# Putting off the first six units' activation, pooling batch 0's keys on TensorE, moving block 1's scaling to GpSimd and batch 1's v pooling among the units

## The chip, the cores and the metric

One core of a Trainium2 chip runs the whole kernel. Its engines are TensorE (PE in the profile, its weight loads PEld), VectorE (DVE), ScalarE (ACT), GpSimd (POOL), and SyncE (SP), whose queue issues nearly all transfers. Each engine works through its own list of instructions in order and waits on semaphores that others raise. The metric is the device time of one execution in microseconds (us).

## What is computed

Three stages in a row, with pooled keys and values in the first:

```
k_p = k.reshape(B, H, Sp, 8, D).mean(axis=3)          # B, H, S, D = 8, 8, 576, 64; Sp = 72
v_p = v.reshape(B, H, Sp, 8, D).mean(axis=3)
attn = softmax(q @ k_p.T / sqrt(D));  x = attn @ v_p  # x: 4608 tokens x 512
h = x @ w_in;  g = h * cos(h);  x = g @ w_out         # w_in 512 x 2048, w_out 2048 x 512
h = x @ w2_in;  s = h * softmax(h);  out = layernorm(s) * g_ln @ w2_out
```

## The kernel before

The tokens are cut into nine blocks of 512 (`NB` = 9, `BLK` = 512; numbered 0 to 8). The program is written out by hand, engine order included: what stands earlier in the code is earlier in each engine's list.

**Beginning.** Before any unit, block 0's attention (`a0`) is run straight through: batch 0's keys are pooled (`add`, L243 to L246: a DVE reduction over eight, and two copies into `kT`), then scores (L426), the exponentials (L441), the scaling by the reciprocal sums (`norm`, L486 and L491), transposes (`e_tr` L522, `e_tr_left` L505) and the products with v (`av`, L549). v of batches 0 and 1 is pooled by matmuls with a 0/1 matrix (`pool_vn`, L287 and L290) and split into parts by `prep_vn`, all before the units.

**Units.** `h = x @ w_in` is made in 72 units, eight to a block. A unit is 24 matmuls (L619) in eight positions of three, into one of three PSUM tiles. Its `chain` has four steps: ACT copies h as a rounded multiple of 2 pi (L630), DVE subtracts that multiple (L633), ACT takes the sine (L636), DVE multiplies by h (L638), which frees the PSUM tile. The steps of a unit run during the next two units; `g_store` then writes the unit to DRAM (`gd`). Among block j-1's units stands block j's attention, at positions that `plan` names, 64 positions to a block: scores and maxima (L391, L399, L400) at 0 to 21, exponentials at 13 and 25, sums and scaling at 16, 19, 28 and 31, the transposes and products from 27 and from 42. The scaling of block 1 (`self.j < 2`) is shared between DVE and POOL, head pair by head pair; later blocks use POOL alone.

**Weights of w_in** arrive as float64 words and are decoded chunk by chunk, 16 chunks, two to a unit of block 0. `pipe.step` does it: ACT prepares (L114, L115), DVE works on the bits (L119, L123, L127), POOL joins them (L139), ACT casts the high part (L1101), POOL subtracts to get the low part (L1102). Through block 0 two steps are run in each unit.

**Last block.** No attention stands among block 8's units. There the weights of the second product are loaded (`w_load`, L856, tiles `ws`) and split by ACT (L163) and POOL (L164); the first two units are read back from `gd` (`g_load`, L653, tiles `gr`), summed (`g_sums`, L664) and split (`g_split`, L675 and L677). The second product (`y_mm`, L702) begins behind the last unit. Its third PSUM bank is the one that the last unit's L638 frees.

Of the kernel before, what the change touches and what calls it, by code (L numbers as in the profile page):

```python
# [19 lines left out]
P = 128  # L20
# [15 lines left out]
def fused_kernel(ctx, tc, qT_d, kT_d, vN_d, vM_d, vL_d, w_in, w_out, w2_in, w2_out, g_ln, out):  # L36
# [183 lines left out]

    def kv_jobs(b, hf):
# [12 lines left out]
        def k_job(i):  # L234
# [45 lines left out]
    def pool_vn(b, hf):  # L280
        if hf == 0:
            pool_vn.ps = ps_y.tile([P, 2, BLK], F32, tag="y", name="vps")
        main, left = pool_vn.ps[:, 0], pool_vn.ps[:, 1]
        t = v_t[b]
        c = slice(4 * D * hf, 4 * D * (hf + 1))
        for i in range(4):
            nc.tensor.matmul(  # L287
                main[:, c], lhsT=pool_w["m"][:, i], rhs=t[i // 2][:, i % 2, c], start=(i == 0),
                stop=(i == 3))
        nc.tensor.matmul(  # L290
            left[:, c], lhsT=pool_w["l"][0:64], rhs=t[2][0:64, 0, c], start=True, stop=True)
        v_t[b, hf] = main, left

    def prep_vn(b, hf):
        main, left = v_t.pop((b, hf))
        vm, vl = vM[b][:, hf], vL[b][:, hf]
        c = slice(4 * D * hf, 4 * D * (hf + 1))
# [3 lines left out]
        nc.vector.tensor_tensor(  # L301
            out=w.rearrange("p (i a d) -> p i a d", i=2, a=2),
            in0=main[:, c].rearrange("p (i a d) -> p i a d", i=2, a=2),
            in1=m_half.rearrange("p (o a u) -> p o a u", o=1, u=1).to_broadcast([P, 2, 2, D]),
            op=ALU.mult,
        )
        for k2, m in enumerate((m_head, m_hlo)):
# [5 lines left out]
        w = w.rearrange("p (i c) -> p i c", i=2)
        nc.scalar.copy(out=vm[:, 0], in_=w)
        nc.scalar.copy(out=hi, in_=u[:, 0])
        nc.gpsimd.tensor_tensor(out=vm[:, 1], in0=w, in1=vm[:, 0].bitcast(F32), op=ALU.subtract)
        nc.vector.scalar_tensor_tensor(
# [1143 lines left out]
```

## Time and profile before

| | |
|---|---|
| device time, median of 3 runs (lowest, highest) | 1356.5 us (1356.32, 1357.1) |
| the profiled execution: device time, span | 1354.56 us, 1352.8 us |
| busy in the span: PE, DVE, ACT, POOL | 1299.7, 1058.2, 697.6, 500.3 us |
| mean granted TensorE clock | 0.988 of full speed |

The span is the time from the first to the last instruction of one execution. Busy times overlap; what counts is where PE has to wait. Units run from 44 us to 563 us of the span, the second product from there to 939 us, the third stage behind it.

### The profile page before, as it was taken

The numbers are of one execution on the slowest core, as the hardware profiler recorded it, in microseconds if no ns is written. First come the engines' busy times: TensorE is split into PE (matmuls) and PEld (weight loads), VectorE is DVE, ScalarE is ACT, GpSimd is POOL, SyncE is SP. The second block draws the span as 40 slices with busy tenths as digits, with TensorE's granted clock in tenths as the row PEclk, the third lists the DMA queues.
The fourth block names the chain that finished last, engine by engine and source line by source line (L and its number), as shares of the span: only waits on it lengthen the run. The fifth ranks groups of instructions, "written<-read, shape, count | busy, mean of one in ns | idle before, by whom it ended". The sixth has DMA issues, their size and how long they took to land. (4 is left out here: it accounts for less than half of the span.)

```text
span 1352.8 us, 20432 instructions
## 1 busy us (share of the span) xinstructions
PE 1299.7 (96%) x7510; PEld 1132.1 (84%) x7510; DVE 1058.2 (78%) x1686; ACT 697.6 (52%) x992; POOL 500.3 (37%) x668
## 2 busy tenths in 40 slices
PE   6879999999999999799999999999999999999998
PEld 4558877887887888699999999999878888888887
DVE  7897887978879684688889999895777767676753
ACT  4576666756557466544444444444444444444432
POOL 3868676665554125230110001001343434343410
PEclk8989999999999999899999999999999999999999
DMA  8425566664665526555455555558501111111101
GB/s 296 155 82 199 192 236 236 236 243 160 236 211 187 185 110 233 183 192 135 148 157 167 164 168 172 160 180 311 191 33 55 39 55 40 55 39 55 40 24 39
DMA packets 81268, 202.93 MB, mean 150 GB/s; under 512 B 7824, under 2 KB 26256, under 8 KB 81168
## 3 DMA queue, kind: packets, MB, share of 16 engines
q1 hardware_dynamic: 81024, 201.62, 44.2%
q8 instruction: 59, 0.97, 0.3%
q14 instruction: 41, 0.34, 0.1%
q10 hardware_dynamic: 144, 0.00, 0.0%
HBM read 124.00 MB, written 77.59 MB: 149 GB/s over the span
## 5 line engine op out<-in xcount | busy, mean ns | idle before, releaser
L619 PE MATMUL h<-x,w 128*128 128x512 f32 x1728 | 435.9, 401 | 1.4 <-DVE t L638 0.8
L702 PE MATMUL y<-g,wy 128*128 128x256 f32 x3024 | 365.8, 284 | 10.9 <-DVE t L638 8.7
L702 PEld LDWEIGHTS y<-g,wy 128*128 128x128 f32 x3024 | 364.8, 193 | 11.9 <-issue 8.8
L619 PEld LDWEIGHTS h<-x,w 128*128 128x128 f32 x1728 | 317.8, 190 | 65.9 <-DVE t L638 1.8
L675 ACT CAST g<-gs 128x1024 fp32r<-128x1024 f32 x72 | 75.7, 1051 | 174.0 <-PE y L702 96.1
L677 DVE TENSOR_TENSOR g<-gs,g 128x1024 fp32r<-128x1024 f32 x72 | 90.2, 1253 | 33.3 <-ACT g L675 33.2
L636 ACT ACTIVATE t<-t,cst 128x1024 f32<-128x1024 f32 x72 | 83.0, 1152 | 63.3 <-DVE t L633 63.2
L139 POOL TENSOR_TENSOR dec<-dec,raw 128x512 int32<-128x512 int32 x24 | 33.9, 1414 | 210.0 <-DVE dec L127 176.4
L638 DVE TENSOR_TENSOR t<-t,h 128x1024 f32<-128x1024 f32 x72 | 87.4, 1214 | 26.1 <-ACT t L636 26.0
L902 POOL TENSOR_TENSOR yl<-yr,yh 128x1024 fp32r<-128x1024 f32 x18 | 43.8, 2433 | 153.5 <-ACT yh L897 153.5
L630 ACT ACTIVATE t<-h 128x1024 int32<-128x1024 f32 x72 | 73.4, 1020 | 49.0 <-PE h L619 48.9
L633 DVE SCALAR_TENSOR_TENSOR t<-t,h 128x1024 f32<-128x1024 int32 x72 | 87.2, 1212 | 5.1 <-ACT t L630 5.1
L231 POOL TENSOR_TENSOR kvraw<-kvraw 128x256 f32<-128x256 f32 (+3 forms) x128 | 82.4, 644 | 9.2 <-DMA kvraw<-in_vM 1.5
L677 DVE TENSOR_TENSOR g<-gr,g 128x768 fp32r<-128x768 f32 x72 | 76.1, 1057 | 0.0
L664 DVE TENSOR_TENSOR gs<-gr,gs 128x256 f32<-128x256 f32 x144 | 71.1, 494 | 5.0
L1033 POOL TENSOR_TENSOR sc<-sc,cst 128x1 f32<-128x1 f32 x36 | 20.3, 564 | 141.5 <-DVE sc L1022 114.1
L1068 ACT COPY o<-o 128x512 f32<-128x512 f32 x36 | 21.1, 587 | 96.4 <-PE o L1086 96.4
L1084 PE MATMUL o<-w,lh 128*128 128x512 f32 x176 | 69.0, 392 | 0.0
L1086 PE MATMUL o<-w,ll 128*128 128x512 f32 x176 | 68.5, 389 | 0.0
L1085 PE MATMUL o<-w,lh 128*128 128x512 f32 x176 | 68.5, 389 | 0.0
L164 POOL TENSOR_TENSOR wy<-ws,wy 128x512 fp32r<-128x512 f32 (+1 forms) x32 | 40.5, 1301 | 61.9 <-ACT wy L163 61.8
L139 POOL TENSOR_TENSOR wf<-dec,raw 128x512 int32<-128x512 int32 x24 | 31.4, 1308 | 83.7 <-DVE dec L127 43.6
(179 smaller groups left out, 2556.7 us busy)
## 6 DMA issues: line engine op xcount, KB each, us to landing
gd<-t SPq DMA_DIRECT2D x72, 512.0 KB, 2.9
gr<-gd SPq DMA_DIRECT2D x72, 512.0 KB, 4.0
raw<-in_w_in SPq DMA_DIRECT2D x24, 512.0 KB, 5.0
raw<-in_w_out SPq DMA_DIRECT2D x24, 512.0 KB, 4.9
kvraw<-in_kT SPq DMA_DIRECT2D x32, 288.0 KB, 4.3
qT<-in_qT SPq DMA_DIRECT2D x36, 256.0 KB, 4.7
yd<-yo SPq DMA_DIRECT2D x36, 256.0 KB, 4.7
yr<-yd SPq DMA_DIRECT2D x18, 512.0 KB, 3.9
```

The costliest lines, as they stand in the source:

```text
L231: nc.gpsimd.tensor_tensor(out=x[:, 0:m], in0=x[:, 0:m], in1=x[:, m:2 * m], op=ALU.add)
L619: nc.tensor.matmul(h_ps[n][:, i], lhsT=w[:, a, kk, :], rhs=x[:, b], start=(kk == 0 and m == 0), stop=(kk == KD - 1 and m == 2),)
L630: nc.scalar.activation(out=t.bitcast(I32), in_=h, func=AF.Copy, scale=1.0 / TWO_PI, bias=0.25)
L633: nc.vector.scalar_tensor_tensor(out=t, in0=t.bitcast(I32), scalar=-TWO_PI, in1=h, op0=ALU.mult, op1=ALU.add)
L636: nc.scalar.activation(out=t, in_=t, func=AF.Sin, bias=halfpi)
L638: nc.vector.tensor_tensor(out=t, in0=t, in1=h, op=ALU.mult)
L664: nc.vector.tensor_tensor(out=o, in0=x, in1=y, op=ALU.subtract)
L675: nc.scalar.copy(out=flat(g[-1])[:, 0:n * NH], in_=flat(f)[:, 0:n * NH])
L677: nc.vector.tensor_tensor(out=flat(g[-1])[:, 0:n * NH], in0=flat(f)[:, 0:n * NH], in1=flat(g[-2])[:, 0:n * NH].bitcast(F32), op=ALU.subtract)
L702: nc.tensor.matmul(y_ps[j][i][:, NH * c:NH * (c + 1)], lhsT=w[:, a, P * c:P * (c + 1)], rhs=g[y][b], start=(q == 0 and c == 0 and k == 0), ...
L1084: nc.tensor.matmul(ps, lhsT=hi, rhs=w[:, 0], start=(c == 0), stop=False)
L1085: nc.tensor.matmul(ps, lhsT=hi, rhs=w[:, 1], start=False, stop=False)
```

## The change

Five edits:

1. Batch 0's keys are pooled by PE: eight matmuls with the identity add up the eight strips of 72 columns in PSUM (a tile of `ps_q`), and DVE copies out of PSUM. The DVE reduction L243 is gone.
2. For units 0 to 5 the four steps of `chain` become one ACT copy from PSUM to a tile, which `g_store` writes to `gd` as plain h. In the last block `put_off` reads each of the six back, does the four steps in SBUF, and writes the result: one load and one store of 512 KB more for each, in two slots of `wo` in turn. Unit n's load stands at position 1 + 8n, its steps 6, 8, 10 and 12 positions behind, its store 14 behind.
3. All of block 1's scaling runs on POOL; in block 0 DVE keeps the odd head pair.
4. `pool_vn` and `prep_vn` of batch 1 leave the beginning. Among block 0's units they stand at positions 1 and 5 (PE), with the DVE, ACT and POOL steps at 3, 4, 6 and 7, 8, 10. Their PSUM tile comes from `ps_a`.
5. In the beginning `e_tr_left(0)` and `e_tr(1)` are written ahead of parts of `norm`.

```diff
             def add():
                 if b == 0:
-                    t = wo.tile([P, SP], F32, "kp")
-                    nc.vector.tensor_reduce(
-                        out=t, in_=raw.rearrange("p (r s) -> p s r", r=POOL), axis=AX.X, op=ALU.add)
+                    if p == 0:
+                        add0.ps = ps_q.tile([P, 2, BLK], F32, tag="q", name="kp")
+                    t = add0.ps[:, 0, SP * p:SP * (p + 1)]
+                    for r in range(POOL):
+                        nc.tensor.matmul(
+                            t, lhsT=ident, rhs=raw[:, SP * r:SP * (r + 1)], start=(r == 0),
+                            stop=(r == POOL - 1))
                     nc.vector.tensor_copy(out=dst[0:D, 0:SP], in_=t[0:D])
...
-                    eng = nc.vector if self.j < 2 and i2 else nc.gpsimd
+                    eng = nc.vector if self.j == 0 and i2 else nc.gpsimd
...
                 for i in range(2):
                     put(i, add, 1, 1, KV[i])
+                    put(1 + 4 * i, pool_vn, 1, i)
+                    staged((3 + 4 * i, 4 + 4 * i, 6 + 4 * i), prep_vn, 1, i)
...
+    NP = 6
+
     def chain(n, step):
+        if n < NP:
+            if step == 0:
+                h_t[n] = gp.tile([P, 2, BLK], F32, tag="t", name="t")
+                nc.scalar.copy(out=flat(h_t[n]), in_=flat(h_ps.pop(n)))
+            return
...
+    def put_off(n, put, o):
+
+        j, q = units[n]
+        t = []
+
+        def load():
+            t.extend(wo.tile([P, 2, BLK], F32, "h", 12 + 2 * (n % 2) + i) for i in range(2))
+            nc.sync.dma_start(out=t[0], in_=gd[j][:, q])
+
+        def step(k):
+            h, g = flat(t[0]), flat(t[1])
+            if k == 0:
+                nc.scalar.activation(
+                    out=g.bitcast(I32), in_=h, func=AF.Copy, scale=1.0 / TWO_PI, bias=0.25)
+            elif k == 1:
+                nc.vector.scalar_tensor_tensor(
+                    out=g, in0=g.bitcast(I32), scalar=-TWO_PI, in1=h, op0=ALU.mult, op1=ALU.add)
+            elif k == 2:
+                nc.scalar.activation(out=g, in_=g, func=AF.Sin, bias=halfpi)
+            else:
+                nc.vector.tensor_tensor(out=g, in0=g, in1=h, op=ALU.mult)
+
+        put(o, load)
+        for k in range(4):
+            put(o + 6 + 2 * k, step, k)
+        put(o + 14, lambda: nc.sync.dma_start(out=gd[j][:, q], in_=t[1]))
...
         pool_vn(0, 0)
         pool_vn(0, 1)
-        prep_vn(0, 0)
+        now(prep_vn(0, 0))
         a0.now("e_tr", 0)
+        a0.now("e_tr_left", 0)
         a0.now("norm", 2)
+        a0.now("e_tr", 1)
+        now(prep_vn(0, 1))
         a0.now("norm", 3)
-        a0.now("e_tr_left", 0)
-        a0.now("e_tr", 1)
-        prep_vn(0, 1)
         a0.now("av", 0)
...
-        pool_vn(1, 0)
         a0.now("e_tr", 3)
         add(1, 0, "k0")
         a0.now("e_tr_left", 1)
-        prep_vn(1, 0)
         a0.now("av", 2)
-        pool_vn(1, 1)
         pipe.step()
-        prep_vn(1, 1)
...
+        for n in range(NP):
+            put_off(n, put_at(NB), 1 + 8 * n)
```

Three places in the engines' lists, in which line numbers shift with the change (L486 and L491, the scaling, become L503 and L508; L1102 becomes L1155; L643, L856 and the chain's L630 and L636 become L669, L909, L656 and L662). First POOL's list at the first scaling in block 0 before the change: joins (`dec`), low parts (`w`), and the even head pair's scaling (`em`, `el`).

```order
L139 TENSOR_TENSOR dec<-dec,raw_163 128x512
L1102 TENSOR_TENSOR w<-dec,w 128x512
L486 TENSOR_TENSOR em<-e,sm 128x4x128
L491 TENSOR_TENSOR el<-e,sm 128x4x32 x2
L139 TENSOR_TENSOR dec<-dec,raw_164 128x512
```

And the same place now:

```order
L139 TENSOR_TENSOR dec<-dec,raw_163 128x512
L1155 TENSOR_TENSOR w<-dec,w 128x512
L503 TENSOR_TENSOR em<-e,sm 128x4x128
L508 TENSOR_TENSOR el<-e,sm 128x4x32 x2
L503 TENSOR_TENSOR em<-e,sm 128x4x128
L508 TENSOR_TENSOR el<-e,sm 128x4x32 x2
L139 TENSOR_TENSOR dec<-dec,raw_164 128x512
```

Both head pairs' scaling now stands in front of the next chunk's join. Next SP's queue in the last block before the change, around the loads of weight pieces 4 and 5 (`ws`) and the stores of units (`gd_119<-t`):

```order
L856 DMA ws<-wf_153 128x1024
L856 DMA ws<-wf_152 128x1024
L643 DMA gd_119<-t 128x1024
L856 DMA ws<-wf_155 128x1024
L856 DMA ws<-wf_154 128x1024
L643 DMA gd_119<-t 128x1024
```

And now, with the put-off loads (`h<-gd_111`) and stores (`gd_111<-h`):

```order
L696 DMA gd_111<-h 128x1024
L909 DMA ws<-wf_153 128x1024
L909 DMA ws<-wf_152 128x1024
L678 DMA h<-gd_111 128x1024
L669 DMA gd_119<-t 128x1024
L696 DMA gd_111<-h 128x1024
L678 DMA h<-gd_111 128x1024
L909 DMA ws<-wf_155 128x1024
L909 DMA ws<-wf_154 128x1024
L669 DMA gd_119<-t 128x1024
L696 DMA gd_111<-h 128x1024
L678 DMA h<-gd_111 128x1024
```

From the first load of weight pieces in the last block to the last row shown there were 18 transfers and are now 28: twelve `ws`, six stores of units, six put-off loads and four put-off stores. Last ACT's list in the last block before the change, one unit and a half of it (`wy` is the weights' split):

```order
L636 ACTIVATE t<-t,cst 128x1024
L630 ACTIVATE t<-h 128x1024
L163 ACTIVATE wy<-ws 128x2x256 x3
L163 ACTIVATE wy<-ws 128x256
L636 ACTIVATE t<-t,cst 128x1024
```

And now, with the put-off first and third steps (L683 and L689) among them:

```order
L662 ACTIVATE t<-t,cst 128x1024
L683 ACTIVATE h<-h 128x1024
L656 ACTIVATE t<-h 128x1024
L163 ACTIVATE wy<-ws 128x2x256 x2
L689 ACTIVATE h<-h,cst 128x1024
L163 ACTIVATE wy<-ws 128x2x256
L163 ACTIVATE wy<-ws 128x256
L662 ACTIVATE t<-t,cst 128x1024
```

The first put-off step, which reads the loaded tile, stands ahead of the next unit's own first step (L656).

## Rows read from the trace of the kernel before

**Rows 1.** Windows: length, busy of PE, PEld, DVE, ACT, POOL; PEclk, DMA share, GB/s

```profile
44.00:121.40 77.40, 62.93 (x288) 49.41 (x289) 67.03 (x94) 48.44 (x70) 58.64 (x66) 0.93 0.40 139
121.40:177.10 55.70, 55.50 (x281) 46.78 (x280) 43.97 (x66) 37.05 (x49) 35.54 (x55) 1.00 0.59 210
519.40:563.20 43.80, 43.80 (x196) 36.28 (x195) 23.12 (x24) 29.28 (x42) 27.04 (x24) 1.00 0.76 260
520.00:550.00 30.00, 30.00 (x134) 24.85 (x133) 14.47 (x12) 22.92 (x36) 23.95 (x22) 1.00 0.98 334
5.40:10.00 4.60, 4.58 (x16) 3.88 (x16) 3.57 (x6) 1.20 (x9) 0.00 (x0) 1.00 1.02 381
```

**Rows 2.** Timeline of PE in block 0: start, length, instructions, [idle before]

```profile
78.24 0.85 PE L522 MATMUL eTp<-ident,em 128*128 128x128 f32 x4 [2.62 <-DVE e L400]
78.74 3.80 PE L619 MATMUL h<-x,w 128*128 128x512 f32 x9
...
87.65 0.66 PE L522 MATMUL eTp<-ident,em 128*128 128x128 f32 x4 [2.60 <-DVE eT L527]
...
93.95 0.52 PE L549 MATMUL xo<-eT,vM 128*128 128x64 f32 x3 [2.27 <-DVE eL L510]
```

**Rows 3.** DVE and POOL groups, 44 to 121.4 us: count | busy us, mean ns

```profile
L633 DVE SCALAR_TENSOR_TENSOR t<-t,h 128x1024 f32<-128x1024 int32 x7 | 8.5, 1211 | 0.0
...
L491 DVE TENSOR_TENSOR el<-e,sm 128x128 f32<-128x128 f32 x4 | 4.0, 1026 | 0.0
...
L486 DVE TENSOR_TENSOR em<-e,sm 128x512 f32<-128x512 f32 x2 | 3.0, 1496 | 0.0
...
L486 POOL TENSOR_TENSOR em<-e,sm 128x512 f32<-128x512 f32 x2 | 2.6, 1289 | 0.0
L491 POOL TENSOR_TENSOR el<-e,sm 128x128 f32<-128x128 f32 x4 | 1.8, 478 | 0.0
```

**Rows 4.** Waits of POOL, 44 to 121.4 us: total us, times, longest

```profile
POOL dec L139 <- DVE dec L127: 14.6, 8, 3.0
```

**Rows 5.** Timeline of ACT in block 0, around the second pair of exponentials

```profile
78.78 0.63 ACT L1101 ACTIVATE w<-dec 128x512 fp32r<-128x512 f32 x1 [0.98 <-POOL dec L139]
80.01 0.70 ACT L114 ACTIVATE dec<-raw 128x512 f32<-128x512 f32 x1 [0.60 <-POOL w L1102]
...
81.32 1.28 ACT L457 ACT_TABLE_LOAD   x1
82.62 1.26 ACT L457 ACTIVATE e<-e 128x576 f32<-128x576 f32 x2
```

**Rows 6.** Timelines of DVE and PE in the beginning

```profile
3.74 1.18 DVE L243 TENSOR_REDUCE kp<-kvraw 128x72 f32<-128x576 f32 x1 [0.16 <-DMA kvraw<-in_kT]
...
5.41 4.58 PE L426 MATMUL sc<-kT,qT 128*128 128x144 f32 x16 [5.41 <-DVE kT L246]
10.62 1.25 PE L426 MATMUL sc<-kT,qT 128*128 128x144 f32 x8 [0.62 <-DVE kT L246]
...
39.62 1.99 PE L287 MATMUL vps<-vn,pool_w 128*128 128x256 f32 x8 [0.50 <-DVE vu L308]
41.54 0.70 PE L290 MATMUL vps<-vn,pool_w 64*128 64x256 f32 x2
...
44.01 0.93 PE L619 MATMUL h<-x,w 128*128 128x512 f32 x3 [0.65 <-DVE vu L308]
```

**Rows 7.** Timeline of ACT in the last block: the first use of a loaded weight piece

```profile
522.01 1.15 ACT L163 ACTIVATE wy<-ws 128x512 fp32r<-128x512 f32 x2 [1.12 <-DMA ws<-wf]
```

**Rows 8.** Timelines of DVE and PE at the end of the last block

```profile
559.89 1.23 DVE L677 TENSOR_TENSOR g<-gs,g 128x1024 fp32r<-128x1024 f32 x1 [2.18 <-ACT g L675]
...
573.33 20.73 PE L702 MATMUL y<-g,wy 128*128 128x256 f32 x158 [8.67 <-DVE t L638]
```

**Rows 9.** Timeline of DVE while POOL splits weights, behind the last block

```profile
591.33 2.32 DVE L677 TENSOR_TENSOR g<-gs,g 128x1024 fp32r<-128x1024 f32 x1
```

**Rows 10.** Groups of DVE instructions, 513 to 565 us

```profile
L638 DVE TENSOR_TENSOR t<-t,h 128x1024 f32<-128x1024 f32 x9 | 11.0, 1218 | 13.8 <-ACT t L636 13.8
```

More of the change, by code (lines that the diff above doesn't have):

```diff
@@ L219, in fused_kernel, with add0 @@
     KV = ("k0", "k1", "v0", "v1", "v2")
+    def add0():
+        pass
     def kv_jobs(b, hf):
@@ L280, in pool_vn @@
     def pool_vn(b, hf):
[L281 to L283 removed]
         t = v_t[b]
         c = slice(4 * D * hf, 4 * D * (hf + 1))
+        if b > 0:
+            ps = ps_a.tile([P, 2, 4 * D], F32, tag="a", name="vps")
+            main, left = ps[:, 0], ps[:, 1]
+        else:
+            if hf == 0:
+                pool_vn.ps = ps_y.tile([P, 2, BLK], F32, tag="y", name="vps")
+            main, left = pool_vn.ps[:, 0, c], pool_vn.ps[:, 1, c]
         for i in range(4):
             nc.tensor.matmul(
[L288 removed]
+                main, lhsT=pool_w["m"][:, i], rhs=t[i // 2][:, i % 2, c], start=(i == 0),
                 stop=(i == 3))
         nc.tensor.matmul(
[L291 removed]
+            left, lhsT=pool_w["l"][0:64], rhs=t[2][0:64, 0, c], start=True, stop=True)
         v_t[b, hf] = main, left
@@ L296, in prep_vn @@
         vm, vl = vM[b][:, hf], vL[b][:, hf]
-        c = slice(4 * D * hf, 4 * D * (hf + 1))
         w = wo.tile([P, 4 * D], F32, "vw")
@@ L300, in prep_vn, with first, second, third @@
         hi = wo.tile([P, 4 * D], F32R, "vh")
[L301 to L307, printed above, removed]
+        w2 = w.rearrange("p (i c) -> p i c", i=2)
+        def first():
             nc.vector.tensor_tensor(
-                out=u[:, k2].rearrange("p (c d) -> p c d", c=4),
-                in0=left[:, c].rearrange("p (c d) -> p c d", c=4),
-                in1=m.rearrange("p (c o) -> p c o", o=1).to_broadcast([P, 4, D]), op=ALU.mult,
-            )
[L313 to L317, printed above, removed]
-            out=vl.rearrange("p i c -> p (i c)"), in0=hi.bitcast(F32), scalar=m_sh, in1=u[:, 1],
-            op0=ALU.mult, op1=ALU.add)
+                out=w.rearrange("p (i a d) -> p i a d", i=2, a=2),
+                in0=main.rearrange("p (i a d) -> p i a d", i=2, a=2),
+                in1=m_half.rearrange("p (o a u) -> p o a u", o=1, u=1).to_broadcast([P, 2, 2, D]),
+                op=ALU.mult,
+            )
+            for k2, m in enumerate((m_head, m_hlo)):
+                nc.vector.tensor_tensor(
+                    out=u[:, k2].rearrange("p (c d) -> p c d", c=4),
+                    in0=left.rearrange("p (c d) -> p c d", c=4),
+                    in1=m.rearrange("p (c o) -> p c o", o=1).to_broadcast([P, 4, D]), op=ALU.mult,
+                )
+        def second():
+            nc.scalar.copy(out=vm[:, 0], in_=w2)
+            nc.scalar.copy(out=hi, in_=u[:, 0])
+        def third():
+            nc.gpsimd.tensor_tensor(out=vm[:, 1], in0=w2, in1=vm[:, 0].bitcast(F32), op=ALU.subtract)
+            nc.vector.scalar_tensor_tensor(
+                out=vl.rearrange("p i c -> p (i c)"), in0=hi.bitcast(F32), scalar=m_sh, in1=u[:, 1],
+                op0=ALU.mult, op1=ALU.add)
+        return first, second, third
     def prep_v(b):
@@ L1104, in c_in, with now @@
         return Chunk(w_in_w[f], done, home)
+    def now(fns):
+        for fn in fns:
+            fn()
     def kv_load(b, hf, *names):
```

2 lines of the change are left out of this document (added).

## Prediction

> **What bounds the kernel now.** I read the stages by windows first, to see where PE is not fed. Units take 55.7 us a block where all goes well: block 1's window is filled by PE to 55.5 us. Block 0 takes 77.4 us for the same 192 matmuls, so 21.7 us are lost there [rows 1]. The last block has no attention and takes 43.8 us with PE busy throughout [rows 1]; behind it PE waits 8.67 us for DVE's last L638 [rows 8]. So the places that the change touches are the first 44 us, block 0's 21.7 us, the last block, which is full, and the wait behind it.
>
> Next the timeline of PE in block 0. The reader is to see waits of 2.3 to 2.6 us, all for DVE [rows 2]: for a score tile that DVE has not read, for a transposed tile (`eT`), for the left part (`eL`). After a wait nine matmuls take 3.80 us where 9 x 43.8 / 192 = 2.05 is the pace; the window's mean granted clock is 0.93, so there are stretches at the lower level of 1.2 GHz, and they follow idle PE. DVE is busy 67.0 of the 77.4 us, POOL 58.6, ACT 48.4 [rows 1]. POOL in turn waits 14.6 us for DVE's bit work before its joins [rows 4]. DVE is the busiest engine of block 0, POOL the next.
>
> In the last block the transfers are the full resource: from 520 to 550 us their share is 0.98 at 334 GB/s [rows 1]. ACT has 29.3 of 43.8 us, DVE 23.1, POOL 27.0.
>
> **The beginning.** Keys: the four DVE reductions of 1.18 us (one is shown) go [rows 6]. In their place PE makes 32 matmuls of 72 columns, which count twice, since the trace records two passes for each fp32 matmul (x16 for eight score instructions). A pass of 144 columns takes 4.58 / 16 = 0.29 us at first and 1.25 / 8 = 0.16 us later [rows 6]; 72 columns lie between half of that and all of it. Sixteen passes for one head pair are thus 2.3 to 4.6 us slow, 1.2 to 2.5 us fast, against 1.18 us on DVE, and the second pair's matmuls, the first copies and the first scores stand in one line on PE. I expect the first scores about 3 us later than at 5.41, and the later ones to catch up, as PE runs on and DVE has 4.7 us less to do. Block 0's v and softmax then run 1 us later or as now. Against that, batch 1's v pooling leaves this stretch: 2 x (1.99 + 0.70) = 5.4 us of PE, and the wait of the first unit for the last read of its PSUM tile, 0.65 us [rows 6]. PE is not full there (5.9 of 8 us just before), so not all of it comes back: I take the first unit 2.4 us earlier. Bounds: 2 us later (pooling slow, nothing regained) and 6 us earlier (all of 5.4 + 0.65).
>
> **Block 0.** Removed from DVE: two operations of 1.21 us in each of six units, 14.5 us, and the odd head pairs' scaling, 3.0 + 4.0 us [rows 3]. So DVE's 67.0 us become about 47. PE gains 5.4 us of v pooling. POOL gains two head pairs' scaling, each 1.29 + 2 x 0.48 = 2.25 us, 4.5 us in all: 63.1 us. That is more than PE's own 55.7 + 5.4 = 61.1 us, so POOL becomes the fullest engine, and block 0 can shrink by at most 77.4 - 61.1 = 16.3 us.
>
> It will shrink by much less, because of where the scaling stands: both pairs are scaled ahead of the next chunk's join, 4.5 us in which no chunk is joined. ACT's cast (L1101) waits for that join, and behind it in ACT's list come the next chunk's preparation, the second pair of exponentials and the transposed tile's cast [rows 5]. So PE's second set of transposes, which now waits until 87.65 [rows 2], still hangs on this chain. Now the join waits for DVE's decode, which stands behind DVE's own scaling (7.0 / 2 = 3.5 us) and a 1.21 us operation of the chain; afterwards it waits for 4.5 us on POOL instead. What is gained there: the table load of 1.28 us [rows 5], since no sine stands between the exponentials, and the chain's operations ahead of the reads of `eT` and `eL`, 1.21 us each; from the waits of 2.60 and 2.27 us [rows 2] I count 2.8 us. Sum 4.1 us: block 0 takes 73.3 us. Bounds: nothing, if POOL's 4.5 us are paid in full twice, and 16.3 us.
>
> **The last block.** Twelve transfers of 512 KB are added to a stage whose transfers are full. In SP's queue 28 instead of 18 stand up to the sixth put-off load (12 weight halves, 6 unit stores, 6 loads, 4 stores). One is 0.524 MB, at 334 GB/s 1.57 us, at the best pace of the beginning, 381 GB/s, 1.38 us [rows 1]. The first landed at 522.0 [rows 7], so the 28th lands 27 x 1.57 = 42.4 us later, at 564.4, or 37.2 us later, at 559.2. The step that reads it stands at position 47 of 64: 519.4 + 47 x 43.8 / 64 = 551.6. It is 7.6 to 12.8 us late; I take 10.5, nearer to the pace of this stage itself. ACT waits at that step with everything behind it: unit 69's first step, and through it the PSUM tile that a later unit needs, the sums and splits of the first units, the last L638. The earlier put-off loads stall PE on the way for the same reason, but that delay is part of this one, not added. At the end DVE had 2.18 us of waiting to spare ahead of the first split [rows 8], and gets one more L638-like operation there, 1.2 us. So the second product begins 10.5 - 2.2 + 1.2 = 9.5 us later, be it as stalls within the block or as a longer wait than 8.67 us behind it. Bounds: 1.2 us if every load is in time, 11.8 us by the slow pace, and 2.2 more if the next paragraph is right.
>
> The operations have another price than in the beginning. With h in PSUM an L638 takes 1.22 us throughout this block, though POOL splits weights beside it for 27 us [rows 1, 10]. A DVE operation of the same size with both inputs in SBUF took 2.32 us beside POOL's splits [rows 9]. The put-off ones have both inputs in SBUF, twelve of them, so up to 12 x 1.1 = 13 us more of DVE, which has 20 us free. Only two stand in the late chain at the end: 2.2 us. The Trainium skill's page SBUF — State Buffer (section Who interferes with whom) says that a DVE instruction with two SBUF inputs and a GpSimd instruction that reads SBUF exclude each other for the whole instruction. By that rule each of the twelve could wait for a whole split; the row just cited agrees in kind. Since the late chain's last operations come when POOL's splits are mostly over, the sum leaves it out.
>
> **The sum.** -2.4 - 4.1 + 9.5 = +3.0 us. Made against the profiled execution's own 1354.56 us it is 1357.6; the median of the runs stands 1.9 us above that execution, so 1356.5 + 3.0 = 1359.5 us. A change of 0.2%, 2.7 us, is about the least that a measurement of this kernel can tell from none.
>
> **Rivals.** (a) *DVE's relief is worth most of block 0's loss.* Every PE wait named in [rows 2] ends on DVE, and DVE loses 20 of 67 us; POOL's waits of 14.6 us for DVE [rows 4] shrink too. If the second exponentials do not hang on the scaling, block 0 falls to 65 us: -2.4 - 12.4 + 9.5 = -5.3, 1351.2 us. It decides at 77.4 - (9.5 - 2.4) = 70.3 us for block 0: below that the kernel is faster. Against it speaks POOL's sum of 63.1 us with its list in order. Chance 0.31.
> (b) *The transfers run at 381 GB/s* [rows 1] *and less is late*: 7.6 - 1.0 = 6.6 us given back, which is 1356.6 us, no change. The best stretch of the beginning is loads alone, the last block mixes stores in. Chance 0.15.
> (c) *The port in the last block*: 2.2 us more, 1361.7 us. Chance 0.10.
> (d) *The beginning gets longer*, since 64 slow passes hold up the first exponentials, and the first unit starts 2 us later instead of 2.4 earlier: 1363.9 us. PE's later passes are at 0.16 us [rows 6], which speaks against it. Chance 0.07.
> The forecast as summed has 0.37.
>
> **Numbers.** Faster comes from (a), 0.29 of its 0.31, and 0.04 of (b) with a somewhat better block 0: 0.33. Slower is 0.27 of the forecast, (c), and 0.05 of (d): 0.42. The rest, 0.25, is within 0.2%. The likeliest case alone spans 1355 to 1364 us. The range must reach through most of (a) and to (d): 1347 to 1367 us.
>
> **What would show it.** Right: block 0 at 72 to 75 us with the first unit near 41.6 us; POOL its fullest engine; PE's longest wait before the transposes in position 33. In the last block ACT waiting for the loads of `h`, in total over 5 us, the block at 46 to 52 us, and L702 resuming some 3 us later than at 573.33. Wrong: block 0 under 70 us; or no ACT wait for `h` loads; or the first scores before 6 us, or the first unit behind 44 us.

## The result and the profile after

| | before | changed |
|---|---|---|
| device time, median of 4 runs each (lowest, highest) | 1356.41 us (1356.2, 1357.1) | 1369.26 us (1368.83, 1373.13) |
| ratio to before, 95% interval | | 1.0104 (1.0091 to 1.0116) |
| profiled execution: device time, span | 1354.56, 1352.8 us | 1373.13, 1371.3 us |

The change makes the kernel 12.9 us slower; 1359.5 was forecast, with 1347 to 1367 as range. The profiled execution of the changed kernel is the longest of its four. A second profile of the same kernel was therefore taken with the experiments (*changed_again*, ratio 1.0113, 1.0098 to 1.0129), and both are read here. The kernel before's profiled execution is 1.9 us below its median, so the spans differ by more than the medians: by 18.5 us in the first profile and 15.4 in the second.

The span falls into five stretches at marks in PE's timeline. Block 0 goes from the first unit's first matmul to the first score matmul that stands among block 1's units (of block 2's attention), blocks 1 to 7 from there to the last product with v, the last block from there until the second product resumes behind its wait for DVE.

| us | before | changed | changed_again |
|---|---|---|---|
| first unit starts | 44.01 | 47.93 | 45.02 |
| block 0 | 78.1 | 78.1 | 78.4 |
| blocks 1 to 7 | 391.5 | 393.3 | 392.4 |
| last block and handover | 59.7 | 73.1 | 73.4 |
| the rest | 779.5 | 778.9 | 778.9 |

So the loss is 1 to 4 us of the beginning and 13.3 to 13.7 us of the last block; block 0, where the change was to pay, is as long as before.

**The beginning.** PE's timeline of the changed kernel: start, length, instructions, [idle before]. The L249 rows are the keys' passes.

```profile
3.88 3.66 PE L249 MATMUL kp<-kvraw,ident 128*128 128x72 f32 x16 [3.88 <-DMA kvraw<-in_kT]
8.11 3.69 PE L249 MATMUL kp<-kvraw,ident 128*128 128x72 f32 x16 [0.57 <-DVE kT L253]
11.59 2.22 PE L443 MATMUL sc<-kT,qT 128*128 128x144 f32 x8
13.60 3.53 PE L249 MATMUL kp<-kvraw,ident 128*128 128x72 f32 x16
...
18.94 2.33 PE L249 MATMUL kp<-kvraw,ident 128*128 128x72 f32 x16
...
28.11 0.66 PE L539 MATMUL eTp<-ident,em 128*128 128x128 f32 x4
...
47.93 1.48 PE L638 MATMUL h<-x,w 128*128 128x512 f32 x3
```

A pass takes 0.22 to 0.23 us in the first three groups. The first scores start at 11.59 us instead of 5.41 [rows 6], and what was meant to catch up does not: PE is busy without a gap from the second group of passes up to the first transposes. In the second profile the third group of passes is faster:

```profile
13.55 2.17 PE L249 MATMUL kp<-kvraw,ident 128*128 128x72 f32 x16
...
25.33 0.66 PE L539 MATMUL eTp<-ident,em 128*128 128x128 f32 x4
```

The transposes then come 2.8 us earlier, and so does the first unit (45.02). The windows show a granted clock of 1.00 over the passes in both profiles, so they do not say why the same passes take 0.22 us (3.53 / 16) in one profile and 0.14 us (2.17 / 16) in the other.

**Block 0.** Windows of the changed kernel over block 0, and over three stretches of the last block (columns as in [rows 1]):

```profile
47.93:126.03 78.10, 68.27 (x313) 53.50 (x311) 59.37 (x85) 42.00 (x67) 66.06 (x73) 0.94 0.44 154
...
525.00:549.00 24.00, 22.69 (x99) 17.89 (x97) 13.16 (x10) 16.72 (x23) 17.21 (x12) 1.00 0.95 329
549.00:555.00 6.00, 0.23 (x1) 0.26 (x2) 2.73 (x3) 3.82 (x5) 1.25 (x2) 0.77 0.97 396
554.70:559.00 4.30, 4.23 (x10) 3.38 (x11) 3.02 (x3) 3.85 (x6) 4.30 (x4) 0.50 0.59 237
```

PE's waits in block 0, which answer to [rows 2]:

```profile
70.36 1.02 PE L408 MATMUL sc<-kT,qT 128*64 128x144 f32 x6 [2.60 <-DVE e L417]
...
93.25 0.66 PE L539 MATMUL eTp<-ident,em 128*128 128x128 f32 x4 [3.23 <-DVE eT L544]
...
98.02 0.59 PE L566 MATMUL xo<-eT,vM 128*128 128x64 f32 x3 [2.02 <-DVE eL L527]
```

The waits at the transposes (2.60 us before) and for `eL` (2.27) still stand. DVE has 59.4 us of work instead of 67.0, not 47. The DVE groups show why, first two of the bit operations on the weights before the change (count | busy us, mean ns | idle before):

```profile
L127 DVE SCALAR_TENSOR_TENSOR dec<-raw,dec 128x512 int32<-128x512 int32 x13 | 10.0, 772 | 0.4
L123 DVE TENSOR_SCALAR dec<-dec 128x512 int32<-128x512 int32 x13 | 9.3, 719 | 0.4
```

and now, with one of the groups that came in with batch 1's v (L333; L321 and L314 took 1.5 and 0.8 us):

```profile
L127 DVE SCALAR_TENSOR_TENSOR dec<-raw,dec 128x512 int32<-128x512 int32 x14 | 15.1, 1075 | 0.5
L123 DVE TENSOR_SCALAR dec<-dec 128x512 int32<-128x512 int32 x13 | 13.0, 998 | 0.4
...
L333 DVE SCALAR_TENSOR_TENSOR vL<-vh,cst,vu 128x256 fp32r<-128x256 f32 x2 | 1.7, 872 | 0.0
```

For thirteen of each that is 13 x (0.303 + 0.279) = 7.6 us more for the same work. With only the scaling moved to POOL (*scaling_alone* below) the means are 833 (L127) and 942 ns (L123), so a part of it comes with POOL's scaling alone. DVE's timeline, one chunk while POOL is idle (it waits from 75.2 to 77.19 us) and the next while POOL works:

```profile
75.81 0.43 DVE L123 TENSOR_SCALAR dec<-dec 128x512 int32<-128x512 int32 x1
76.27 0.69 DVE L127 SCALAR_TENSOR_TENSOR dec<-raw,dec 128x512 int32<-128x512 int32 x1
...
78.81 1.41 DVE L123 TENSOR_SCALAR dec<-dec 128x512 int32<-128x512 int32 x1
80.25 1.42 DVE L127 SCALAR_TENSOR_TENSOR dec<-raw,dec 128x512 int32<-128x512 int32 x1
```

POOL and ACT over the second stretch, which is the chain that the prediction drew:

```profile
79.89 1.22 POOL L503 TENSOR_TENSOR em<-e,sm 128x512 f32<-128x512 f32 x1
...
83.25 0.94 POOL L508 TENSOR_TENSOR el<-e,sm 128x128 f32<-128x128 f32 x2
84.15 1.48 POOL L139 TENSOR_TENSOR dec<-dec,raw 128x512 int32<-128x512 int32 x1
```

```profile
85.66 0.64 ACT L1154 ACTIVATE w<-dec 128x512 fp32r<-128x512 f32 x1 [2.35 <-POOL dec L139]
...
88.52 1.24 ACT L474 ACTIVATE e<-e 128x576 f32<-128x576 f32 x2
89.67 0.56 ACT L543 CAST eT<-eTp 128x512 fp32r<-128x512 f32 x1
```

POOL scales for 4.26 us ahead of the join; ACT's cast, the second exponentials and the cast of the transposed tile follow it, then DVE's part of `eT`, and PE at 93.25.

The slow bit operations are what the Trainium skill's page SBUF — State Buffer (section Who interferes with whom) describes: a DVE instruction with two SBUF inputs, or a `tensor_scalar` in a mode with two ports, and GpSimd shut each other out for the whole instruction. The 0.43 against 1.41 us of L123 agree in kind.

**The last block.** PE's timeline, which answers to [rows 8]:

```profile
542.70 5.72 PE L638 MATMUL h<-x,w 128*128 128x512 f32 x24 [0.73 <-DVE t L664]
554.77 18.64 PE L638 MATMUL h<-x,w 128*128 128x512 f32 x72 [6.35 <-DVE t L664]
573.72 5.72 PE L638 MATMUL h<-x,w 128*128 128x512 f32 x24 [0.30 <-DVE t L664]
...
581.09 1.46 PE L755 MATMUL y<-g,wy 128*128 128x256 f32 x10 [1.42 <-DVE g L730]
592.39 3.97 PE L755 MATMUL y<-g,wy 128*128 128x256 f32 x17 [9.84 <-DVE t L664]
```

SP's queue ahead of the 6.35 us, and ACT with its waits for the first weight piece, the third put-off load and the sixth:

```profile
539.17 0.32 SPq L696 DMA_DIRECT2D gd<-h  x1
540.33 3.29 SPq L909 DMA_DIRECT2D ws<-wf  x2
543.67 0.42 SPq L678 DMA_DIRECT2D h<-gd  x1
```

```profile
527.71 1.16 ACT L163 ACTIVATE wy<-ws 128x512 fp32r<-128x512 f32 x2 [1.08 <-DMA ws<-wf]
...
551.18 1.06 ACT L683 ACTIVATE h<-h 128x1024 int32<-128x1024 f32 x1 [6.18 <-DMA h<-gd]
552.14 1.00 ACT L656 ACTIVATE t<-h 128x1024 int32<-128x1024 f32 x1
...
570.04 1.06 ACT L683 ACTIVATE h<-h 128x1024 int32<-128x1024 f32 x1 [0.46 <-DMA h<-gd]
```

The third put-off load needs the tile that the first put-off unit frees with its L691, which ended at 539.15. Its store leaves at 539.17. The row of 3.29 us behind it is two weight loads, each issued in 0.32 us, and a wait between them: SP waits for POOL's splits of earlier weight pieces (L164) to free the tiles. SP's waits from 539.3 to 544 us (us in total, times, longest):

```profile
SPq L909 <- POOL wy L164: 3.3, 2, 2.6
```

So of the 4.5 us between the store and the put-off load, 3.3 are waits for POOL. The load leaves at 543.67 and lands 7.4 us later. ACT waits 6.18 us with the next unit's L656 behind it, and PE waits for the PSUM tile that this unit's chain frees.

### The profile page after: what moved, and what is told of

Same layout as the page of the kernel before. It is cut to its first block, busy times and chain, and to the rows that moved or that the text cites. A ratio compares the mean times of both kernels' runs of the same rounds, so it can differ in the third digit from the quotient of the medians.

```text
span 1371.3 us, 20603 instructions
## 1 busy us (share of the span) xinstructions
PE 1314.8 (96%) x7574; PEld 1146.8 (84%) x7574; DVE 1058.1 (77%) x1676; ACT 700.7 (51%) x996; POOL 512.1 (37%) x674
## 5 line engine op out<-in xcount | busy, mean ns | idle before, releaser
L638 PEld LDWEIGHTS h<-x,w 128*128 128x128 f32 x1728 | 319.5, 191 | 75.2 <-issue 9.3
L662 ACT ACTIVATE t<-t,cst 128x1024 f32<-128x1024 f32 x66 | 76.0, 1152 | 60.1 <-DVE t L659 59.9
L664 DVE TENSOR_TENSOR t<-t,h 128x1024 f32<-128x1024 f32 x66 | 80.1, 1214 | 13.8 <-ACT t L662 13.8
L656 ACT ACTIVATE t<-h 128x1024 int32<-128x1024 f32 x66 | 67.2, 1018 | 42.8 <-PE h L638 42.8
L659 DVE SCALAR_TENSOR_TENSOR t<-t,h 128x1024 f32<-128x1024 int32 x66 | 80.0, 1212 | 0.0
L717 DVE TENSOR_TENSOR gs<-gr,gs 128x256 f32<-128x256 f32 x144 | 72.1, 501 | 5.0
L730 DVE TENSOR_TENSOR g<-gr,g 128x768 fp32r<-128x768 f32 x72 | 74.5, 1035 | 0.1
L164 POOL TENSOR_TENSOR wy<-ws,wy 128x512 fp32r<-128x512 f32 (+1 forms) x32 | 46.8, 1493 | 68.5 <-ACT wy L163 37.7
```

Of the source, the lines that this page charges most:

```text
L638: nc.tensor.matmul(h_ps[n][:, i], lhsT=w[:, a, kk, :], rhs=x[:, b], start=(kk == 0 and m == 0), stop=(kk == KD - 1 and m == 2),)
L659: nc.vector.scalar_tensor_tensor(out=t, in0=t.bitcast(I32), scalar=-TWO_PI, in1=h, op0=ALU.mult, op1=ALU.add)
L662: nc.scalar.activation(out=t, in_=t, func=AF.Sin, bias=halfpi)
L664: nc.vector.tensor_tensor(out=t, in0=t, in1=h, op=ALU.mult)
L717: nc.vector.tensor_tensor(out=o, in0=x, in1=y, op=ALU.subtract)
L730: nc.vector.tensor_tensor(out=flat(g[-1])[:, 0:n * NH], in0=flat(f)[:, 0:n * NH], in1=flat(g[-2])[:, 0:n * NH].bitcast(F32), op=ALU.subtract)
```

## The experiments

Each kernel's median stands against the kernel before on the same chip. Lengths are those of the table above, from one profile each. Line numbers differ by a few between versions.

| label | median, before, us | ratio (95%) | first unit | block 0 | last block |
|---|---|---|---|---|---|
| keys_dve | 1367.86, 1354.74 | 1.0097 (1.008 to 1.0114) | 42.67 | 78.1 | 74.5 |
| scale_shared | 1369.80, 1354.74 | 1.0116 (1.0101 to 1.0131) | 45.80 | 80.1 | 71.9 |
| no_put_off | 1358.53, 1354.74 | 1.0035 (1.002 to 1.0049) | 47.86 | 80.5 | 59.7 |
| put_off_block7 | 1364.60, 1354.74 | 1.0075 (1.006 to 1.009) | 47.83 | 77.5 | 59.9 |
| changed_again | 1371.05, 1355.68 | 1.0113 (1.0098 to 1.0129) | 45.02 | 78.4 | 73.4 |
| keys_alone | 1359.18, 1355.68 | 1.0029 (1.0018 to 1.004) | 49.11 | 78.8 | 59.7 |
| v_late_alone | 1357.63, 1355.68 | 1.0016 (1.0007 to 1.0026) | 41.23 | 81.5 | 59.8 |
| raw_fix | 1370.77, 1355.68 | 1.011 (1.0095 to 1.0125) | 48.17 | 77.8 | 72.1 |
| two_put_off | 1358.86, 1356.14 | 1.0017 (1.0005 to 1.003) | 45.00 | 79.8 | 61.0 |
| three_put_off | 1363.5 (one run), 1356.14 | | 44.92 | 79.7 | 67.7 |
| spread_alone | 1354.19, 1356.14 | 0.9989 (0.9978 to 1.0) | 44.67 | 75.1 | 59.8 |
| scaling_alone | 1355.64, 1356.14 | 0.9993 (0.9982 to 1.0004) | 45.72 | 76.7 | 59.7 |
| v_late_fix | 1357.91, 1355.90 | 1.0016 (1.0007 to 1.0026) | 41.61 | 81.6 | 59.8 |
| scaling_and_spread | 1353.60, 1355.90 | 0.999 (0.998 to 1.0001) | 44.30 | 74.9 | 59.8 |
| spread_no_keys | 1355.16, 1355.90 | 0.9998 (0.9989 to 1.0007) | 42.16 | 77.8 | 59.8 |

**keys_dve**: from the changed kernel, edit 1 undone.

```diff
-                    if p == 0:
-                        add0.ps = ps_q.tile([P, 2, BLK], F32, tag="q", name="kp")
-                    t = add0.ps[:, 0, SP * p:SP * (p + 1)]
-                    for r in range(POOL):
-                        nc.tensor.matmul(
-                            t, lhsT=ident, rhs=raw[:, SP * r:SP * (r + 1)], start=(r == 0),
-                            stop=(r == POOL - 1))
+                    t = wo.tile([P, SP], F32, "kp")
+                    nc.vector.tensor_reduce(
+                        out=t, in_=raw.rearrange("p (r s) -> p s r", r=POOL), axis=AX.X, op=ALU.add)
```

> The changed kernel with batch 0's keys pooled on DVE again, everything else kept. Theory (the matmul passes of the keys are what delays the beginning): in the changed kernel the key passes took 0.23 us each and the transposes began 6.5 us later than before; without them the first unit starts at 41 to 42 us instead of 47.9, and the kernel takes about 6 us less than the changed one (1363). Rival (the beginning is late because of the waits that follow, the 4.39 us for DVE's x and what was reordered there): the first unit still starts at 45 us or later, and the time falls by less than 3 us.

The first unit starts at 42.67 us, near what the theory has. The time is 13.1 us above before, against 12.9 and 15.4 in the two measurements of the changed kernel, so the 6 us were not there: the rival's size of the gain holds, not its cause. Beside the second profile of the changed kernel (span 1368.2, here 1366.7) 2.3 us come from the first unit and 1.3 from blocks 0 to 7; 1.0 is given back in the last block and 1.1 in the rest. keys_alone shows the edit's price without the others.

**scale_shared**: edit 3 undone.

```diff
-                    eng = nc.vector if self.j == 0 and i2 else nc.gpsimd
+                    eng = nc.vector if self.j < 2 and i2 else nc.gpsimd
```

> The changed kernel with block 1's scaling shared between DVE and POOL again. Theory (the scaling on POOL eats the relief of block 0): in the changed kernel POOL scaled from 79.9 to 84.15 us, the join behind it came late, so did ACT's second exponentials and the transposes, PE waited 3.23 and 2.02 us; with it shared block 0 falls from 77.4 to 72 to 74 us and the kernel takes about 4 us less than the changed one (1365). Rival 1 (DVE's relief is worth nothing, whoever scales): block 0 stays within 1 us of 77.4. Rival 2 (DVE needs the relief of the scaling as well): block 0 gets longer, 79 to 81 us.

The theory falls and rival 2 holds: block 0 is 80.1 us, 1.7 to 2.0 longer. POOL's chain above is real, but sharing the scaling puts as much or more into DVE's list.

**no_put_off**: edit 2 undone.

```diff
-    NP = 6
+    NP = 0
```

> The changed kernel with no unit put off (all six chains where they stood before). Theory: the last block and its handover return to 59.9 us (13.3 us back), and block 0 pays with the chain's twelve DVE operations, 4 to 9 us more than 77.4; together 4 to 9 us faster than the changed kernel (1360 to 1365). Rival (the chain's operations in block 0 were hidden, its length is POOL's): block 0 stays at 77 to 78.5 us and the kernel is 12 to 13 us faster than the changed one, about 1357.

The last block returns to 59.7 us. Block 0 pays 2.1 to 2.4 us, between theory and rival. So the put-off relieves block 0 by some 2.2 us for 14.5 us of DVE work.

**put_off_block7**: the six put-off units' work stands among block 7's units.

```diff
-            put_off(n, put_at(NB), 1 + 8 * n)
+            put_off(n, put_at(NB - 1), 1 + 10 * n)
-            t.extend(wo.tile([P, 2, BLK], F32, "h", 12 + 2 * (n % 2) + i) for i in range(2))
+            t.extend(wo.tile([P, 2, BLK], F32, "h") for i in range(2))
```

> The changed kernel with the six put-off units worked on among block 7's units instead of block 8's, ten positions apart, in the ring of tiles. Theory (the last block's loss is its full transfer queue: the third put-off load is issued late, behind a store and weight loads, and ACT waits 6.18 us for it): in block 7, where the transfers ran at 134 GB/s, no load is late, the last block returns to about 60 us with its handover, block 7 pays at most 2 us, and the kernel takes 11 to 13 us less than the changed one (1356 to 1358). Rival (it is the work itself, 12 ACT and 12 DVE operations in an order that PE waits for): block 7 gets 5 us longer or more, and at most 7 us come back.

The last block returns, but the seven blocks take 400.3 us, 7 to 8 us more than in the changed kernel. The rival holds. Windows of this kernel in block 7:

```profile
490.00:500.00 10.00, 8.16 (x40) 6.15 (x39) 9.83 (x16) 8.15 (x9) 2.85 (x3) 1.00 0.46 171
500.00:510.00 10.00, 7.04 (x27) 5.53 (x26) 9.93 (x13) 6.21 (x9) 5.23 (x6) 0.83 0.73 265
```

DVE is at 9.8 and 9.9 of 10 us, and PE loses 4.8 of 20 us there. With a unit's work every ten positions DVE is the fullest engine; that it sets the length is read from these windows, no run tests it.

**changed_again**: the changed kernel, unaltered.

> The changed kernel once more, unaltered, so that the others of this group stand beside it on one chip: a second profile of it. Theory (TensorE's rise to 2.4 GHz in the beginning comes at different times in different executions): the first unit starts anywhere from 45.5 to 48 us, as it did in the variants so far that share its beginning (45.80, 47.83, 47.86), with block 0 and the last block within 1.5 us of what the first profile showed (78.1 us; 73.1 us from the last product with v to the resumed second product). Rival: it repeats the first profile, 47.9 us.

The first unit starts at 45.02 us, a little ahead of the theory's range and far from the rival's 47.9. The beginnings of the same code stand in two groups, 44.9 to 45.8 and 47.8 to 48.2 us, four profiles in each, by when the passes become faster (13.5 or 18.9 us). The expectation put this down to the level of TensorE's clock; the granted clock is 1.00 there in both profiles, so that is not shown.

**keys_alone**: the kernel before with edit 1 only (its lines as in the diff of the change).

> The kernel before with only the keys of batch 0 pooled on PE. Theory (the passes are slow, 0.23 us each, and delay everything behind the first scores): the first unit starts 3 to 6 us later than 44.0 us and the kernel takes 3 to 6 us more than before, 1358 to 1361 on the clock of the last group's chip. Rival (what is lost in the beginning is caught up in block 0, since undoing this edit in the changed kernel started the first unit 5.3 us earlier, but the kernel got only about 1 us faster): the first unit 3 to 6 us later, block 0 shorter by as much, the time within 1.5 us of before.

The theory holds: first unit at 49.11, 5.1 us late, block 0 not shorter (78.8), the kernel 3.5 us slower. (Single profiles: the beginning of the kernel before stands unaltered in *spread_alone*, *scaling_alone* and *scaling_and_spread* too, and starts the first unit there at 44.67, 45.72 and 44.30 us, so that 3.4 to 5.1 us are late.) So nothing is caught up in block 0.

**v_late_alone**: the kernel before with edits 4 and 5 only.

> The kernel before with only batch 1's v pooled among the units and the order of the beginning that goes with it. Theory (a weight chunk's load on SP waits for the tile that batch 1's v holds until PE has pooled it; q of block 1 is queued behind it): the first unit starts about 1.5 us earlier, at 42 to 43 us, SP waits some 15 us for the pooling, PE waits 3 to 4.5 us for q at the score matmuls of the third head pair, block 0 is 3 to 5 us longer than 78.1, and the kernel is 1 to 4 us slower than before. Rival (SP's queue has time, only 5.4 us of PE move from one place to the other): block 0 at most 2 us longer, the kernel within 1 us of before or faster.

First unit 2.8 us earlier, block 0 3.4 us longer, the kernel 2.0 us slower. The wait of PE for q and SP's wait for the pooling are both there:

```profile
63.65 0.91 PE L401 MATMUL sc<-kT,qT 128*64 128x144 f32 x6 [2.89 <-DMA qT<-in_qT]
```

SP's waits (us in total, times, longest):

```profile
SPq L109 <- PE vps L291: 15.8, 1, 15.8
```

Whether they are the cause is what the next two test.

**raw_fix** (on the changed kernel) and **v_late_fix** (on v_late_alone): the same line.

```diff
-        early = {7: raws[1], 9: raws[2], 11: raws[3]}
+        early = {7: raws[1], 8: raws[2], 9: raws[3]}
```

> The changed kernel with three of the early weight chunks loaded to other tiles (chunks 7, 8 and 9 to the raw tiles that the first chunks leave, 11 to its own), so that none of them waits for the tiles that hold batch 1's v. Theory (SP's queue is held up by that wait of 15.6 us): the two loads of q (L396) are issued before 58 us instead of 63.2 and 64.3, the wait of PE at 70.4 us shrinks by at least 2 us, block 0 falls by 2 to 4 us, and the kernel is 2 to 4 us faster than the changed one. Rival (the chunks behind them, which must be decoded in turn, are late anyway, and POOL's list sets the length): block 0 stays within 1 us and so does the kernel.

The theory falls. The line does not take all of SP's wait away: 6.1 us of waiting for batch 1's pooling are left of 15.6, beside 8.3 us for POOL's joins. SP still issued the loads of q only at 61.66 and 62.61 us, but that was soon enough: PE's wait at the third pair's scores shrinks to 0.80 us. Block 0 stays at 77.8 us, for the wait goes elsewhere:

```profile
68.53 0.91 PE L408 MATMUL sc<-kT,qT 128*64 128x144 f32 x6 [0.80 <-PE h L638]
...
93.22 1.12 PE L539 MATMUL eTp<-ident,em 128*128 128x128 f32 x4 [4.63 <-DVE eT L544]
```

> The kernel before with batch 1's v pooled among the units and with the weight chunks' loads turned so that none waits for the tiles of that v. Theory 1 (the 3.4 us of block 0 are the work that came in: 5.4 us of PE, and on DVE 4 us and slower bit operations): PE's wait for q is gone, but block 0 still is 80 to 82 us, with another wait that has grown; the kernel within 1 us of v_late_alone, 1 to 3 us slower than before. Theory 2 (SP's queue): block 0 falls to 78 to 79 us and the kernel is as fast as before or 1 us faster.

Theory 1 holds. Block 0 is 81.6 us without the wait for q. In its place the wait before the first transposes has grown from 0.59 to 2.60 us; before the second it is 2.84 us (3.36 in v_late_alone). So the late loads of q are not what makes block 0 longer. What is left is the work that came in, 5.4 us of PE and some 4 us of DVE; which of it costs the 3.4 us no run separates.

**two_put_off**, **three_put_off**: `NP = 2` and `NP = 3` in the changed kernel.

> The changed kernel with two units put off instead of six. Theory (the third load is the first that needs a tile which an earlier put-off unit gives back, so it stands in SP's queue behind that unit's store and behind weight loads that go out slowly; with two units there is no such load): PE waits under 1 us within the last block, from the last product with v to the resumed second product 60 to 62 us (73.1 in the changed kernel); block 0 79 to 81 us. The kernel takes 9 to 11 us less than the changed one. Rival (the lateness grows with the amount of transfers, a third of it is a third of the loss): 64 us, and 8 us less.

> The changed kernel with three units put off. Theory (queue order): the whole wait for the third load is there, ACT waits 5 to 7 us for it, PE 4 to 7 us for DVE's last step in the middle of the block, and the stretch from the last product with v to the resumed second product is 66 to 70 us. Rival (the amount of transfers and of work): half of the loss, with no single wait of PE over 3 us, 66 us or less.

With two units PE waits 0.69 us within the block and the last block takes 61.0 us; with three it is 67.7 us. The theory holds in both. PE's timelines, of two, then of three, and ACT's of three:

```profile
538.77 27.48 PE L638 MATMUL h<-x,w 128*128 128x512 f32 x120 [0.69 <-DVE t L664]
```

```profile
549.71 23.56 PE L638 MATMUL h<-x,w 128*128 128x512 f32 x96 [4.78 <-DVE t L664]
```

```profile
546.12 1.06 ACT L683 ACTIVATE h<-h 128x1024 int32<-128x1024 f32 x1 [4.60 <-DMA h<-gd]
```

One more load costs 6.7 us, and ACT waits 4.60 us for it, a little less than expected. The loss does not grow in step with the amount of transfers, it begins with the third load, which stands in the queue behind a store and two weight loads; here too SP waits 3.3 us for POOL between the store and the load. How much of the lateness is that place, and how much the 7 us from issue to landing, no run separates. The other three units cost 5.4 us more between them.

**spread_alone**, **scaling_alone**, **scaling_and_spread**: the kernel before with edit 2, edit 3, and both, the six units placed one in each of blocks 2 to 7.

```diff
+        for n in range(NP):
+            put_off(n, put_at(3 + n), 44)
```

> The kernel before with only the put-off edit, and the six units worked on one in each of blocks 2 to 7, at position 44, instead of all in the last block; their tiles come from the ring. Theory (the relief of block 0 is real, 2.2 us in the changed kernel, and only the place of the work costs): block 0 is 75 to 77 us instead of 78.1, the seven blocks behind it at most 1 us longer, the last block as before; 1 to 3 us faster than before. Rival 1 (DVE's order in the blocks is tight): each of the six blocks is 1 to 1.5 us longer, as block 7 paid 9 us for six units, and the kernel is 4 to 7 us slower. Rival 2: no change, since block 0's length hangs on the decoding of the weights and not on the units' steps.

> The kernel before with only block 1's scaling moved to POOL. Theory (the changed kernel got 1.7 to 2 us longer in block 0 when the scaling was shared again): block 0 is 76 to 77 us instead of 78.1 and the kernel 1 to 2 us faster than before. Rival (POOL's 4.4 us ahead of the next join cost as much as DVE gains as long as the units' steps are still in DVE's list): block 0 within 1 us of 78.1, no change. Rival 2: block 0 is 2 us or more longer, since the second exponentials hang on that join.

> The kernel before with the scaling of block 1 on POOL and the six units put off and spread over blocks 2 to 7. Theory 1 (both take work from DVE and the gains add): block 0 is 73 to 74 us (75.06 and 76.73 alone, 78.1 before), the kernel 2.5 to 4 us faster than before. Theory 2 (POOL's 4.4 us ahead of the next join cost what DVE gains once the units' steps are gone): block 0 75 us or more, the kernel no faster than with the spread alone, 2 us faster than before.

The spread holds block 0 at 75.1 us with the last block as before. The kernel is 2.0 us faster than before by the medians, with an interval that just reaches no change. The seven blocks take 1.2 us more, but so they do in scaling_alone, whose edit does not touch them; this is not shown to be the spread's price. Scaling alone gives 76.7 us in block 0 and no change that can be measured in the time. Together they give 74.9 us: theory 2, the two do not add. POOL is then the fullest engine, and the wait before the second set of transposes has grown:

```profile
44.30:119.15 74.85, 61.11 (x291) 47.77 (x292) 52.46 (x77) 40.17 (x63) 63.77 (x71) 0.98 0.46 156
```

```profile
86.40 1.12 PE L522 MATMUL eTp<-ident,em 128*128 128x128 f32 x4 [4.65 <-DVE eT L527]
```

At 0.999 (0.998 to 1.0001), 2.3 us below before, scaling_and_spread is no faster than spread_alone, and its interval reaches no change as well. None of the kernels here is shown to be faster than before.

**spread_no_keys**: the changed kernel without edit 1, with the spread and with the line of raw_fix.

> The changed kernel without the keys on PE, with the six units spread over blocks 2 to 7 and with the weight chunks' loads turned. Theory (the beginning gains 1.3 to 2.8 us from the late v, block 0 loses what it gains by the rest, the last block is as before): first unit 41 to 42.5 us, block 0 77.5 to 78.5 us, the kernel 1 to 3 us faster than before. Rival (the late v costs as much as it gains): within 1 us of before.

The rival holds: first unit 42.16 us, block 0 77.8 us, the time as before. Beside scaling_and_spread, which lacks edits 4 and 5, the first unit is 2.1 us earlier and block 0 2.9 us longer: what the late v gains ahead of the first unit, it gives back behind it.

## Why the prediction was wrong, by its steps

**The beginning, -2.4 us forecast, +1.0 and +3.9 measured.** The part on batch 1's v was right in size: with edit 5, but without the others, it starts the first unit 2.4 to 2.8 us earlier (v_late_fix, v_late_alone; what edit 5 does by itself no run shows). The step that failed is "the first scores about 3 us later" and "the later ones to catch up, as PE runs on". The passes for two head pairs stand ahead of the first scores, which start 6.2 us later. The keys' 64 passes take 13.2 us of PE in the first profile and 11.4 in the second, all ahead of the first transposes, against four DVE reductions of 1.18 us of which PE waited out only a part. Alone the edit costs 5.1 us at the first unit. This was rival (d), with chance 0.07, on whose account "PE's later passes are at 0.16 us" was held against it; in one of two profiles 48 of the 64 passes were at 0.22 us or more. The first unit behind 44 us, which the prediction named as a sign of being wrong, stands in both.

**Block 0, -4.1 us forecast, 0.0 and +0.3 measured.** The two edits that relieve DVE are worth about what was summed: taking them out of the changed kernel one at a time lengthens block 0 by 2.1 to 2.4 and 1.7 to 2.0 us, and together on the kernel before they give 3.2. What failed is that edit 4's arrival in block 0 had no price. Its 5.4 us of PE stood only in a floor of 61.1 us, and its instructions on DVE, ACT and POOL nowhere. With edit 5 alone beside it, it makes block 0 3.4 us longer, and -3.2 + 3.4 = +0.2 is what was measured. The step "DVE's 67.0 us become about 47" failed too (its own terms, 14.5 + 7.0 off 67.0, make 45.5): it is 59.4 us, 7.6 of the difference because L123 and L127 are slower beside a busier POOL, and 3.5 from v's steps (1.7 + 1.5 + 0.8, less 0.5 that stood there before). Rival (a), with block 0 at 65 us, rested on that figure; no run has block 0 under 74.9 us. The chain from the scaling over the join to the transposes in position 33 was right, and 3.23 us stand there; POOL is the fullest engine of the block behind PE, with 66.1 us.

**The last block, +9.5 us forecast, +13.3 and +13.7 measured.** That loads of `h` come late and ACT holds the next units up behind them was right. The step that failed is which load and why: the sixth of 28 transfers at a given rate was counted, and it is the third, by its place in SP's queue behind a store that waits for the same DVE step as its tile, and behind two weight loads for which SP waits 3.3 us for POOL. The sixth load does land as counted at 334 GB/s, 42.3 us after the first weight half (ACT at 527.71 and 570.04), but that is luck: waits of SP and stretches of 329 and 396 GB/s make it up, and ACT waits only 0.46 us for it. Rival (b), a faster rate, is not tested by any run; its "6.6 us given back" is what would remain of the loss, by which its 1356.6 us is right. PE's waits in the block are 0.73 + 6.35 + 0.30 = 7.4 us. The handover, from the second product's first matmul to its resumption, is 13.1 instead of 10.3 us, 2.8 more, where the forecast had -2.2 + 1.2 = -1.0: DVE has no waiting to spare ahead of its first split any more, and the chain of the last units ends later behind the sums and the put-off steps. Most of the remaining 3 us is PE's pace: after the wait 72 matmuls took 18.64 us where 72 x 0.228 = 16.4 is the pace. The first ten of them, until 559 us, ran at a granted clock of 0.50, which is the lower level of 1.2 GHz, behind the 6.35 us in which PE was idle. The price of a wait in the clock was not in the sum. The units of the block end 54 us after the first, not 46 to 52.

**Rival (c), DVE's put-off steps slower beside POOL's splits,** was rightly left out of the sum. Rows of DVE's timeline beside POOL's splits and behind them:

```profile
537.17 1.98 DVE L691 TENSOR_TENSOR h<-h 128x1024 f32<-128x1024 f32 x1
...
568.18 2.01 DVE L691 TENSOR_TENSOR h<-h 128x1024 f32<-128x1024 f32 x1
...
576.14 1.22 DVE L691 TENSOR_TENSOR h<-h 128x1024 f32<-128x1024 f32 x1
```

The two in the late chain, at 568.18 and 576.14 us, took 2.01 and 1.22 us, 0.8 more in all instead of 2.2.

**The sum.** The terms measured are +1.0 to +3.9, 0.0 to +0.3, and +13.3 to +13.7, with +0.9 to +1.8 in the seven blocks between. In both profiles 1.6 us of these fall in block 2, and not by an edit, as the last section tells.

## What to carry to other kernels

When a step is moved into a full stage, price all of its instructions there, on every engine, before counting what it frees where it came from. A load that reuses a tile stands in its queue behind whatever frees that tile and behind every wait of the loads between, so find the first load of that kind before multiplying transfers by a rate. Work taken from DVE and given to POOL comes back in part as longer DVE operations, so measure the busy time that is left and don't subtract.

## What the hardware showed beyond that

- A merged row of a queue can hide a wait. The rows of 1.00 us (at 523.45) and 3.29 us (at 540.33) for two weight loads on SP are two issues of 0.32 us each with a wait between them, for PE in the first and for POOL in the second. Among the twelve weight loads of the last block an issue took 0.32 us in the median and 1.33 at most.
- 16 fp32 passes of 72 columns took 3.53 or 2.17 us at the same point of two executions of one program, at a granted clock of 1.00 in both, and the first unit moved by 2.9 us with it. The Trainium skill's page TensorE: Matmul & The Clock Gate (Part 1) says that the moment at which the engine reaches its higher clock after the start varies between runs of one kernel. The two profiles fit that in kind, but their granted clock does not show a rise, so the cause stays open.
- One and the same wait of PE stands in block 2 in all 17 profiles, 1.89 to 1.94 us before the second transposes. Over the 3.6 us behind it the granted clock was 0.53 to 0.59 in eight of them, where nine matmuls took 3.6 to 3.9 us and the block 60.8, and 1.00 in nine, where they took 2.3 us and the block 59.3. The window behind the wait in scaling_alone, whose edit does not touch block 2, then in the kernel before:

```profile
210.58:214.18 3.60, 3.60 (x12) 2.87 (x11) 3.47 (x4) 2.56 (x5) 2.56 (x6) 0.55 0.96 345
```

```profile
210.22:213.82 3.60, 3.60 (x22) 3.17 (x21) 3.47 (x4) 2.75 (x6) 2.56 (x6) 1.00 0.97 347
```

So the length of a wait does not settle whether the clock falls, and 1.6 us between two single profiles need no edit.
- A DVE `tensor_scalar` of 128x512 took 0.43 us with POOL idle and 1.41 us with POOL working.
